# Tiny matmuls at the head of the TensorE program, and a transpose issued ahead of the output weights: one change to a fused attention and SwiGLU kernel

## The chip, the cores and the metric

The kernel runs on one core of one Trainium2 chip. A core has five engines that run their own programs and meet at semaphores: TensorE (PE in the profile) multiplies matrices into PSUM, VectorE (DVE) and ScalarE (ACT) work on SBUF and PSUM, GpSimd (POOL) works on SBUF, and SyncE (SP) issues transfers. PEld is TensorE's loading of the stationary operand. Transfers between HBM and SBUF run on 16 DMA engines; here nearly all loads and all DMA transposes are issued from SP's queue, in the order of its program, and the results from ScalarE's.

The metric is the device time in microseconds of the whole kernel, the median of several runs.

## What is computed

The inputs are q, k and v of 4 batches, 8 heads, 768 positions and 64 features, a decay `lam` per head, and three weight matrices: gate and value (512 x 1536) and out (1536 x 512). The reference runs an attention without softmax in blocks of 64 positions, with a state that decays, and then a gated feed-forward block:

```python
intra = np.einsum('bhic,bhjc->bhij', qb, kb) * Dmask[None]      # Dmask = lam ** (i - j), i >= j
intra = np.einsum('bhij,bhjd->bhid', intra, vb)
inter = np.einsum('bhid,bhde->bhie', qb * lam_pow[None], kv_state)
out[:, :, sl] = intra + inter
kv_state = lam_block * kv_state + np.einsum('bhsd,bhse->bhde', kb * rev_pow[None], vb)
...
g = x @ w_gate                                                   # x: attention output, 3072 x 512
return (g * (1.0 / (1.0 + np.exp(-g))) * (x @ w_val)) @ w_out
```

The 3072 rows are the 4 x 768 positions, the 512 columns the 8 heads of 64 features.

## The kernel before

The attention is cut into 12 groups of 256 positions of one batch; the state of a batch is carried from its group i to its group i + 1. Two groups make one tile t of 512 rows of the feed-forward block, so there are six tiles. The order of the work is written out by hand: nothing is scheduled by a planner. Each engine executes its instructions in the order in which this code issues them, so a call that is moved is moved on every engine that it uses.

One group g goes through these calls:

- `load_group` (L243): k, q and v from HBM by SP (L99 for groups 0 to 5, L106 for later ones).
- `cast_scaled` (L255): ScalarE casts k (L258), VectorE or GpSimd scales q (L260), and then SP issues `dma_transpose` (L248, L251) of both into `qkt`. Groups 0 to 2 use `pe_transpose` on TensorE (L289) in its place.
- `v_scale` (L235, L238): GpSimd scales v into `v_s`.
- `upd_mm` (L366, L382): TensorE forms the update of the state from k and `v_s`; `upd_copy` (L390) brings it to SBUF with ScalarE; `state` (L410, L421 to L432) adds it up on GpSimd and leaves `kvn`, the state in the middle of the group.
- `scores` (L308, L326): TensorE forms q times k; VectorE multiplies by the causal mask (L333).
- `core_a` (L490) with `inter` (L450, L461): q times the state, on TensorE, with `kv` and `kvn`; `core_b` (L495) with `intra` (L467, L474): scores times `v_s`; then `evac` (L481) copies the result to `xt`, the input of the feed-forward block. `ahead(g)` (L555) is `upd_mm`, `upd_copy`, `state` and `scores` in one.

The feed-forward block of tile t has 12 steps fc. A step is `ffn_gate` (L508, matmuls L514, silu on ScalarE L518) and `ffn_val` (L520, matmuls L528, product on VectorE L531), which give `h`. Then `ffn_out(t, b)` (L538, matmuls L547, copy L549, store L550) multiplies `h` by w_out for each of four blocks b of 128 rows, 12 matmuls each; matmul fc needs columns fc of w_out. Steps are numbered by `step` (L671), and `at(n, fn, ...)` (L675) hangs a call behind step n. The loop at L766 issues step after step and what hangs behind it. s0 are the steps of tile 0; tile 1 runs its 12 steps twice, on the first half of its rows (s1a) and on the second (s1b).

The weights come as float32 and are cast to bfloat16 in the core: gate and value in pieces by `w_piece` and `w_cast` (L206, L218), on ScalarE and GpSimd; out in six pieces of 512 KB by `wo_piece` and `wo_cast` (L225, L230), pieces 0 to 4 on GpSimd and piece 5 on ScalarE (L735). Before the change all six are issued at step s1a[3] behind the loads of group 5, and `cast_scaled(5)`, with its transpose, follows at s1b[3]. On GpSimd the order at the end of tile 1 is: pieces 0 and 1, `state(4)`, pieces 2 and 3, `v_scale(5)`, piece 4.

At the head, `warm_up` (L127) issues matmuls of 128x512 on constants. Four of them lead TensorE's program, then comes `lam_ps` (L163), a product that spreads `lam` over the partitions and from which ScalarE makes the decay tables, then three more. `warm_into` (L165) puts further matmuls on constants between the first stages. PSUM is used as a ring of eight banks.

The last call of the program, `ffn_out` with `last=True` (L542), splits its 512 columns: the first part is copied and stored by ScalarE, the second copied by VectorE and stored by SP.

Of the kernel before, what the change touches and what calls it, by code (L numbers as in the profile page):

```python
# [19 lines left out]
@with_exitstack  # L20
def kernel(
    ctx: ExitStack,
    tc: tile.TileContext,
    q: bass.AP,
    k: bass.AP,
    v: bass.AP,
    lam: bass.AP,
    moe_w_gate: bass.AP,
    moe_w_val: bass.AP,
    moe_w_out: bass.AP,  # L30
    out: bass.AP,
):
    nc = tc.nc
    with tc.manual_schedule():
        _body(ctx, tc, nc, q, k, v, lam, moe_w_gate, moe_w_val, moe_w_out, out)


def _body(ctx, tc, nc, q, k, v, lam, moe_w_gate, moe_w_val, moe_w_out, out):
    B, H, S, D = q.shape
# [3 lines left out]
    DM = H * D  # L43
    DFF = moe_w_gate.shape[1]
    MC = DM // 128
    FC = DFF // 128
# [32 lines left out]
    def bank():  # L79
        b = banks[ring[0] % 8]  # L80
        ring[0] += 1
        return b
# [41 lines left out]
    warm = nc.const_aps.tensor(1.0, [128, 512], BF16)  # L124
    ones = const.tile([1, 128], FP32, name="ones")
    nc.vector.memset(ones, 1.0)
    def warm_up(n, cols=512):  # L127
        b = bank()
        for _ in range(n):
            nc.tensor.matmul(b[:, 0:cols], warm[:, 0:128], warm[:, 0:cols], start=True, stop=True)  # L130
# [28 lines left out]
           for b in range(B)]  # L159

    lam_ps = bank()
    warm_up(4)
    nc.tensor.matmul(lam_ps[:, 0:H], ones[:, 0:128], lam_row, start=True, stop=True)  # L163
    warm_up(3)
    def warm_into(b, n, cols=256):  # L165
        for _ in range(n):
            nc.tensor.matmul(b[:, 0:cols], warm[:, 0:128], warm[:, 0:cols], start=True, stop=True)
# [370 lines left out]
    def ffn_out(t, b, last=False):  # L538
        h_sb = st[("h", t)]
        osb = osb_pool.tile([128, DM], FP32, name="osb", tag="osb")  # L540
        row = groups[2 * t + b // 2][0] * S + (groups[2 * t + b // 2][1] * 2 + b % 2) * BLK
        halves = ((0, DM // 2, nc.scalar.copy, nc.scalar), (DM // 2, DM, nc.vector.tensor_copy, nc.sync)) \  # L542
            if last else ((0, DM, nc.scalar.copy, nc.scalar),)
        for c0, c1, fn, eng in halves:
            ps = bank()[:, 0:c1 - c0]
            for fc in range(FC):
                nc.tensor.matmul(ps, h_sb[:, fc, b], wo_sb[:, fc, c0:c1],  # L547
                                 start=(fc == 0), stop=(fc == FC - 1))
            fn(out=osb[:, c0:c1], in_=ps)  # L549
            eng.dma_start(out=bass.AP(tensor=out.tensor, offset=out.offset + row * DM + c0,  # L550
                                      ap=[[DM, 128], [1, c1 - c0]]),
                          in_=osb[:, c0:c1])
# [118 lines left out]
    def step(t, fc, b0=0, b1=B):  # L671
        steps.append((t, fc, b0, b1))
        return len(steps) - 1

    def at(n, fn, *a):  # L675
        plan.setdefault(n, []).append((fn, a))

    s0 = {fc: step(0, fc) for fc in range(2, FC - 1)}
# [5 lines left out]
    at(s0[3], swapped_q_table)  # L684
    at(s0[4], w_cast)
    at(s0[4], state, 1)
    at(s0[4], load_group, 2, "v")
    at(s0[5], load_group, 3)
    at(s0[6], w_cast)
    at(s0[7], load_group, 4, "kq")  # L690
# [2 lines left out]
    at(s0[8], pe_transpose, 2, 0)  # L693
    at(s0[8], pe_transpose, 2, 1)
    at(s0[8], w_cast)
    at(s0[8], v_scale, 2, nc.gpsimd)
    at(s0[9], scores, 2)
    at(s0[9], run_later, 4)
    at(s0[10], upd_mm, 2)
# [7 lines left out]
    s1a = [step(1, fc, 0, 2) for fc in range(FC)]  # L707
    s1b = [step(1, fc, 2, 4) for fc in range(FC)]
    at(s1a[3], cast_scaled, 4)
    at(s1a[3], load_group, 5)  # L710
    for c in range(0, FC, 2):
        at(s1a[3], wo_piece, c, c + 2)
    at(s1a[7], scores, 3, (0,))
    at(s1a[7], run_later, 2)
    at(s1a[8], scores, 3, (1,))
# [4 lines left out]
    at(s1a[10], core_b, 3, SPLIT)  # L720
    at(s1a[10], v_scale, 4, nc.gpsimd)
    at(s1a[10], state, 3)
    at(s1b[3], cast_scaled, 5)
    at(s1b[3], load_group, 6)
    at(s1b[4], wo_cast)
    at(s1b[4], wo_cast)
    at(s1b[6], ahead, 4)
    at(s1b[6], run_later, 2)
    at(s1b[6], wo_cast)
    at(s1b[6], wo_cast)  # L730
    at(s1b[6], v_scale, 5, nc.gpsimd)
    at(s1b[8], wo_cast)
    at(s1b[9], core_a, 4)
    at(s1b[10], core_b, 4)
    at(s1b[10], wo_cast, ACTC)  # L735
    at(s1b[11], ffn_out, 0, 0)
    at(s1b[11], ahead, 5)
    at(s1b[11], run_later, 3)
    at(s1b[11], ffn_out, 0, 1)
    at(s1b[11], core_a, 5)  # L740
    at(s1b[11], ffn_out, 0, 2)
    at(s1b[11], core_b, 5)
    at(s1b[11], cast_scaled, 6)
# [62 lines left out]
```

## Time and profile before

| what | value |
|---|---|
| median of 13 runs | 228.37 us |
| lowest to highest | 227.87 to 230.0 us |
| the profiled execution: its own time | 229.31 us |
| its span, first to last instruction | 227.6 us |
| TensorE busy | 218.6 us (96%) |
| VectorE, ScalarE, GpSimd busy | 89.5, 107.4, 88.0 us |
| HBM read, written | 28.31 MB, 6.29 MB |
| granted TensorE clock, mean | 0.997 |

The profile is of one execution. Times in it count from the first instruction. A line of a timeline reads: start, length, engine, line of the kernel, operation, output from inputs, shape, how many instructions are put together, and in brackets how long the engine was idle before and what ended that. SPq and ACTq are the engines' queues of transfer issues; the length there is the time of the issue, and the landing of the data comes later. "issue" as a cause is time in which an engine waited for nothing that the profile shows. Busy time of TensorE includes the overlap of neighbouring matmuls, so a busy TensorE can still be sped up or slowed down. The profile also has a row for each 40th of the span, with the share of the DMA engines: they are busy without a break from the second slice to the twelfth (5.7 to 68 us), and mostly under half busy afterwards.

### The profile page before, as it was taken

To read this page: it belongs to the slowest core of one execution; us is meant where nothing else is said; L and a number is where in the kernel's file an instruction comes from. 1 tells how busy PE (TensorE), PEld (TensorE's weight loads), DVE (VectorE), ACT (ScalarE), POOL (GpSimd) and SP (SyncE) were. 2 spreads that over 40 slices of the span, in tenths; PEclk is the share of its full clock that TensorE was granted. 3 is DMA by queue.
4 is the path that set the end of the run, shared out by engine and by line. 5 is a ranking of instruction groups with operands and counts; after the bars stand their busy time and mean duration, and the time that the engine had idled before them with its cause. 6 is when DMAs were issued, how large, how long until landed. Compare 5 with 4: busy or idle time off the path is not lost.

```text
span 227.6 us, 5902 instructions
## 1 busy us (share of the span) xinstructions
PE 218.6 (96%) x2443; PEld 118.1 (52%) x2443; DVE 89.5 (39%) x151; ACT 107.4 (47%) x209; POOL 88.0 (39%) x131
## 2 busy tenths in 40 slices
PE   8789999999997999999999999999999999999994
PEld 3556456878853544454544544544544444444443
DVE  2664347685924213644352361353242123222200
ACT  5868585745562446454354363454433423322221
POOL 6676737641595132976373092092160000000000
PEclk9999999999999999999999999999999999999998
DMA  6999999999997877878889748915101101101122
GB/s 195 346 360 382 366 356 296 213 243 311 348 202 182 235 161 193 200 169 210 201 197 201 190 96 193 229 42 138 49 3 48 46 3 46 46 0 46 49 92 92
DMA packets 88012, 39.70 MB, mean 174 GB/s; under 512 B 57650, under 2 KB 83506, under 8 KB 87986
## 3 DMA queue, kind: packets, MB, share of 16 engines
q1 hardware_dynamic: 83474, 32.64, 55.4%
q10 hardware_dynamic: 4512, 6.69, 8.2%
q8 instruction: 19, 0.31, 0.6%
q14 instruction: 7, 0.06, 0.1%
HBM read 28.31 MB, written 6.29 MB: 152 GB/s over the span
## 4 chain that ended last, share of the span: by engine, by line
PE 82%; DMA 5%; SPq 5%; POOL 5%; issue 1%; ACT 0%; DVE 0%; DVEq 0%; POOLq 0%
PE bank L547 27%; PE bank L514 25%; PE bank L528 24%; SPq L99 4%; DMA woraw<-in_moe_w_out_dram 3%; DMA v<-in_v_dram 2%; POOL wo_sb L232 2%; POOL v_s L238 2%; PE bank L474 2%; PE bank L461 2%; PE bank L382 1%; PE bank L352 1%; SPq L227 1%; POOL kvf L421 1%; PE bank L326 0%
## 5 line engine op out<-in xcount | busy, mean ns | idle before, releaser
L531 DVE TENSOR_TENSOR h<-sil,bank 128x512 bf16<-128x512 bf16 (+1 forms) x87 | 51.3, 595 | 106.2 <-PE bank L528 90.4
L514 PE MATMUL bank<-xt,wg_sb 128*128 128x512 bf16 (+1 forms) x348 | 76.6, 343 | 0.0
L528 PE MATMUL bank<-xt,wv_sb 128*128 128x512 bf16 (+1 forms) x348 | 76.4, 342 | 0.0
L547 PE MATMUL bank<-wo_sb,h 128*128 128x512 bf16 (+1 forms) x300 | 65.8, 371 | 1.8 <-POOL wo_sb L232 1.8
L518 ACT ACTIVATE sil<-bank 128x512 bf16<-128x512 f32 (+1 forms) x87 | 45.8, 527 | 44.3 <-PE bank L514 41.3
L528 PEld LDWEIGHTS <-wv_sb 128*128 128x128 bf16 x348 | 34.0, 98 | 28.3
L547 PEld LDWEIGHTS <-h 128*128 128x128 bf16 x300 | 29.1, 98 | 34.3 <-issue 2.1
L514 PEld LDWEIGHTS <-wg_sb 128*128 128x128 bf16 x348 | 32.4, 98 | 27.2 <-DVE xt L486 0.3
L549 ACT COPY osb<-bank 128x512 f32<-128x512 f32 (+1 forms) x24 | 13.9, 577 | 54.5 <-PE bank L547 52.5
L238 POOL TENSOR_TENSOR v_s<-v,dec 128x1024 bf16<-128x1024 f32 (+1 forms) x14 | 23.3, 1667 | 16.3 <-DMA v<-in_v_dram 13.3
L421 POOL TENSOR_TENSOR kvf<-kvs,ups 128x256 f32<-128x256 f32 x8 | 5.8, 727 | 42.5 <-ACT ups L404 42.5
L333 DVE TENSOR_TENSOR ssb<-bank,causal 128x512 bf16<-128x512 f32 x24 | 15.3, 684 | 4.1 <-PE bank L326 4.0
L486 ACT CAST xt<-bank 128x512 bf16<-128x512 f32 x21 | 12.8, 663 | 2.9 <-PE bank L474 2.4
L430 POOL CAST kvn<-kvf 64x256 bf16<-64x256 f32 x24 | 12.5, 519 | 1.5
L421 POOL TENSOR_TENSOR kvf<-kvf,ups 128x256 f32<-128x256 f32 x16 | 11.6, 726 | 0.7
L260 DVE TENSOR_TENSOR qk<-qraw,qdn 128x1024 bf16<-128x1024 f32 x6 | 7.8, 1306 | 7.1 <-DMA qraw<-in_q_dram 3.7
L404 ACT COPY ups<-bank 128x256 f32<-128x256 f32 (+1 forms) x24 | 9.5, 449 | 2.4 <-PE bank L382 1.5
L258 ACT CAST qk<-kraw 128x1024 bf16<-128x1024 f32 x9 | 9.4, 1042 | 0.5 <-DMA kraw<-in_k_dram 0.5
L357 DVE TENSOR_TENSOR ssb<-bank,causaln 128x512 bf16<-128x512 f32 x12 | 8.3, 688 | 1.2 <-PE bank L352 1.1
L232 POOL CAST wo_sb<-woraw 128x1024 bf16<-128x1024 f32 x5 | 5.2, 1042 | 7.3 <-DMA woraw<-in_moe_w_out_dram 7.3
L221 POOL CAST wv_sb<-wraw 128x1024 bf16<-128x1024 f32 (+1 forms) x6 | 5.8, 971 | 5.3 <-DMA wraw<-in_moe_w_val_dram 5.2
L474 PE MATMUL bank<-ssb,v_s 64*64 64x128 bf16 (+1 forms) x384 | 6.8, 208 | 0.5 <-ACT guard L445 0.5
(63 smaller groups left out, 116.7 us busy)
## 6 DMA issues: line engine op xcount, KB each, us to landing
out_dram<-osb ACTq DMA_DIRECT2D x23, 256.0 KB, 2.1
v<-in_v_dram SPq DMA_DIRECT2D x16, 256.0 KB, 4.2
woraw<-in_moe_w_out_dram SPq DMA_DIRECT2D x6, 512.0 KB, 8.6
kraw<-in_k_dram SPq DMA_DIRECT2D x24, 128.0 KB, 3.4
qraw<-in_q_dram SPq DMA_DIRECT2D x24, 128.0 KB, 3.7
wraw<-in_moe_w_gate_dram SPq DMA_DIRECT2D x5, 512.0 KB, 7.2
wraw<-in_moe_w_val_dram SPq DMA_DIRECT2D x5, 512.0 KB, 6.9
kraw<-in_k_dram SPq DMA_DIRECT2D x4, 512.0 KB, 7.0
```

The costliest lines, as they stand in the source:

```text
L238: eng.tensor_tensor(out=st[("vs", g)][:, h0:h1], in0=st[("v", g)][:, h0:h1].rearrange("p h (s d) -> p h s d", s=2), in1=vfac(g, h0, h1), o ...
L333: nc.vector.tensor_tensor(out=ssb[:, h2, 2 * c:2 * c + 2].rearrange("p a s n -> p a (s n)"), in0=sp[(c, h2)].rearrange("p (a x) -> p a x", ...
L421: nc.gpsimd.tensor_tensor(out=o, in0=f, in1=u, op=ALU.add)
L430: nc.gpsimd.tensor_copy(out=o[64 - h2 * 64:128 - h2 * 64], in_=f[h2 * 64:h2 * 64 + 64])
L474: nc.tensor.matmul(op[r][h2 * 64:h2 * 64 + 64, cols(g, hp, s)], v_s[ps, 2 * hp + h2, s], ssb[ps, h2, hp * 2 + s] if g >= NAT0 else ssb[ps, ...
L486: fns[r](out=xt[:, g % 2, :, r].rearrange("p h (m s) -> p h s m", s=2) if g < NAT0 else xt[:, g % 2, :, :, r * M:r * M + M], in_=op[r].rea ...
L514: nc.tensor.matmul(gp[:, 0:N], wg_sb[:, mc, fs], xt[:, b0 // 2:b1 // 2, mc].rearrange("p g b n -> p g (b n)"), start=(mc == 0), stop=(mc = ...
L518: nc.scalar.activation(sil[:, 0:N], gp[:, 0:N], AF.Silu)
L528: nc.tensor.matmul(vp[:, 0:N], wv_sb[:, mc, fs], xt[:, b0 // 2:b1 // 2, mc].rearrange("p g b n -> p g (b n)"), start=(mc == 0), stop=(mc = ...
L531: nc.vector.tensor_tensor(out=h_sb[:, fc, b0:b1].rearrange("p b n -> p (b n)"), in0=sil[:, 0:N], in1=vp[:, 0:N], op=ALU.mult)
L547: nc.tensor.matmul(ps, h_sb[:, fc, b], wo_sb[:, fc, c0:c1], start=(fc == 0), stop=(fc == FC - 1))
L549: fn(out=osb[:, c0:c1], in_=ps)
```

## The change

There are five edits.

- At the head, four matmuls of 128x512 are replaced by 78 matmuls with a stationary operand of 64x64 and 8 moving columns, on the lower and upper half of the rows in turn; the lam product follows directly, and five matmuls of 128x512 (before: three) follow that.
- `load_group(2, "v")` becomes two loads of half the heads, and `v_scale(2)` becomes two instructions of half the heads.
- Only piece 0 of w_out is issued at s1a[3]. `cast_scaled(5)`, with the transpose of group 5, moves from s1b[3] to s1b[0]; pieces 1 to 5 of w_out follow behind it, then the loads of group 6.
- `v_scale(5)` moves behind the last w_out cast on GpSimd.
- The last store is split at column 384 instead of 256.

On GpSimd the order at the end of tile 1 becomes: pieces 0 and 1, `state(4)`, pieces 2, 3 and 4, `v_scale(5)`. On SP it becomes: loads of group 5, piece 0, transpose of group 5, pieces 1 to 5, loads of group 6. TensorE's program grows from 4,885 to 5,037 instructions.

```diff
     lam_ps = bank()
-    warm_up(4)
+    b = bank()
+    for n in range(78):
+        r = slice(n % 2 * 64, n % 2 * 64 + 64)
+        nc.tensor.matmul(b[r, 0:8], warm[r, 0:64], warm[r, 0:8], start=True, stop=True, skip_group_check=True)
     nc.tensor.matmul(lam_ps[:, 0:H], ones[:, 0:128], lam_row, start=True, stop=True)
-    warm_up(3)
+    warm_up(5)
...
-        halves = ((0, DM // 2, nc.scalar.copy, nc.scalar), (DM // 2, DM, nc.vector.tensor_copy, nc.sync)) \
+        halves = ((0, DM - 128, nc.scalar.copy, nc.scalar), (DM - 128, DM, nc.vector.tensor_copy, nc.sync)) \
             if last else ((0, DM, nc.scalar.copy, nc.scalar),)
...
-    at(s0[4], load_group, 2, "v")
+    at(s0[4], load_fp32, 2, nc.sync, v, "v", 0, H // 2)
+    at(s0[4], load_fp32, 2, nc.sync, v, "v", H // 2, H)
...
-    at(s0[8], v_scale, 2, nc.gpsimd)
+    at(s0[8], v_scale, 2, nc.gpsimd, 0, H // 2)
+    at(s0[8], v_scale, 2, nc.gpsimd, H // 2, H)
...
     at(s1a[3], cast_scaled, 4)
     at(s1a[3], load_group, 5)
-    for c in range(0, FC, 2):
-        at(s1a[3], wo_piece, c, c + 2)
+    at(s1a[3], wo_piece, 0, 2)
...
-    at(s1b[3], cast_scaled, 5)
-    at(s1b[3], load_group, 6)
+    at(s1b[0], cast_scaled, 5)
+    for c in range(2, FC, 2):
+        at(s1b[0], wo_piece, c, c + 2)
+    at(s1b[0], load_group, 6)
     at(s1b[4], wo_cast)
     at(s1b[4], wo_cast)
     at(s1b[6], ahead, 4)
     at(s1b[6], run_later, 2)
     at(s1b[6], wo_cast)
     at(s1b[6], wo_cast)
-    at(s1b[6], v_scale, 5, nc.gpsimd)
     at(s1b[8], wo_cast)
+    at(s1b[8], v_scale, 5, nc.gpsimd)
```

## The prediction

> **What bounds the kernel now.** I read the busy shares first, then what TensorE (PE) waits for, then the chain that ended last, then the timelines around the places the diff names. PE is busy 218.6 of the 227.6 us span, and the table of stretches puts its idle time before 16 us (3.3 us), between 48 and 70 us (1.8 us) and in crumbs of about 0.3 us a group after that. So a change pays only where PE stands still, and a new PE wait is paid in full. PE's own waits:
>
> ```profile
> engine line waited for: us in total, times, longest us
> PE bank L547 <- POOL wo_sb L232: 1.8, 1, 1.8
> ...
> PE bank L167 <- issue: 0.7, 1, 0.7
> ```
>
> The large one is the first output product (`ffn_out(0, 0)`, L547) waiting for the fifth cast piece of w_out. The chain that ended last (start, length, what) shows what that wait stands on:
>
> ```profile
> 53.03 7.54 DMA woraw<-in_moe_w_out_dram
> 60.63 1.04 POOL wo_sb L232
> 61.67 0.70 POOL kvf L421
> ...
> 66.63 1.88 POOL v_s L238
> 68.50 0.99 POOL wo_sb L232
> 69.54 1.02 PE bank L547 x4
> ```
>
> The landing of piece 1 of w_out (53.03 + 7.5 = 60.5) starts a stretch in which GpSimd (POOL) never rests until 69.49: cast of piece 1, state of group 4, pieces 2 and 3, v scale of group 5, piece 4. SP's own timeline in that stage, transposes (L251), loads (L99) and w_out pieces (L227):
>
> ```profile
> 41.36 2.10 SPq L251 DMA_TRANSPOSE qkt<-qk  x1
> 43.53 0.57 SPq L99 DMA_DIRECT2D v<-in_v_dram  x1
> 45.67 2.25 SPq L251 DMA_TRANSPOSE qkt<-qk  x1
> 47.96 0.59 SPq L99 DMA_DIRECT2D kraw<-in_k_dram  x1
> ...
> 51.59 4.62 SPq L227 DMA_DIRECT2D woraw<-in_moe_w_out_dram  x6
> 58.51 8.16 SPq L251 DMA_TRANSPOSE qkt<-qk  x1
> ```
>
> Today all six pieces are issued ahead of group 5's transpose. The same stage on POOL and PE, where the state of group 4 is handed over:
>
> ```profile
> 62.42 0.40 POOL L432 CAST kvn<-kvf 128x256 bf16<-128x256 f32 x1
> 62.81 0.30 PE L461 MATMUL bank<-qkt,kv 64*64 64x128 bf16 x2
> 62.89 0.22 PE L461 MATMUL bank<-qkt,kvn 64*64 64x128 bf16 x1
> ```
>
> `kvn` is done at 62.82 and PE uses it at 62.89. There is no slack between piece 1 and PE.
>
> **The change, part by part. 1: w_out behind the transpose.** Five pieces move on SP's queue past one transpose, and that transpose waits for `cast_scaled(5)`, which moves from step s1b[3] to s1b[0]. VectorE (DVE) finishes the product of s1b[0] at 54.62; q of group 5 was issued at 48.61 and lands 6.0 later, 54.6. So its scaling (1.22) ends at 55.84, and by the row of 44.31 + 1.22 -> 45.67 the transpose is issued 0.14 later, 55.98. SP then has nothing to issue from 52.99 to there. ScalarE's cast of k (landed 48.0 + 5.2 = 53.2) fits at 54.07; the eight PSUM banks let PE run about three steps (2.6 us) ahead of both engines, so it doesn't feel the 1.2 us.
>
> The issue of a transpose takes 2.1 to 2.25, so piece 1 can't be issued before about 58.1 (53.03 today). When does it land? Two rows show a 512 KB load issued directly behind a transpose: v of group 4, 41.36 -> 43.53 + 4.4 = 47.9, that is 6.5 after the transpose's issue; k of group 5, 45.67 -> 53.2, that is 7.5, with more loads behind it as here. I take the middle, 7.0. Part 2 brings the casts 0.2 forward, so the transpose is issued at 55.8 and piece 1 lands at **62.8 (62.3 to 63.3)** instead of 60.5.
>
> POOL's program waits for it in order: behind cast 1 stand the state of group 4, casts 2 to 4 and now last the v scale. Two things follow. `kvn` comes 2.3 after the landing (62.82 - 60.53), at 65.1, and PE, due at `inter(4)` at 62.6, stands about 2.5 us. That isn't the end of it, since POOL is the engine behind: from the start of cast 1 to the end of the stretch it works 8.86 today (60.63 to 69.49), the same instructions in the new order. With 0.1 from landing to start and 0.05 to PE, the v scale is done and `upd_mm(5)` (L382) starts at landing + 9.0 = **71.8**. Today it starts at 70.49. The later stall takes in the earlier: PE, 2.5 us late, reaches the output product at 68.1, finds piece 4 cast at 69.9, just when its turn comes, ends it near 70.7, and waits 1.1 more for the v scale. Pieces 2 to 4 land about 1.4 us apart and are cast later than that; piece 5, on ScalarE, lands near 68.5, is cast by about 69.7 and used at 70.2.
>
> Cost: 71.8 - 70.49 = **+1.3**, bounds +0.8 and +1.8 by the two rows. No PE wait behind 71 us can give it back (the idle there is 2.5 us in 156, inside the groups). The transposed group 5 comes at about 60 instead of 70.3, and the group 6 loads leave SP earlier; both only gain slack, since `scores(5)` at 70.9 didn't wait.
>
> **Cast before v scale (POOL).** By itself it would remove the 1.77 wait, and then `upd_mm(5)` would wait for the v scale instead, due at 69.49: at most 0.95 won. Its whole effect is in the 9.0 above.
>
> **2: the head.** PE stops for no cause shown at 13.9 to 14.73, and further on is bound by a cast:
>
> ```profile
> 14.73 0.27 PE L167 MATMUL bank<-const-bfloat16-1.0 128*128 128x256 bf16 x1 [0.68 <-issue]
> 18.98 1.04 POOL L221 CAST wv_sb<-wraw 128x1024 bf16<-128x1024 f32 x1 [2.06 <-DMA wraw<-in_moe_w_val_dram]
> 20.33 1.03 PE L528 MATMUL bank<-xt,wv_sb 128*128 128x512 bf16 x4
> ```
>
> The instruction queue moved 19 packets, 0.31 MB, for 4,886 PE instructions, 257 each, and the first packet inside the span lies in the stretch 12.0 to 13.3, just ahead of the stop. So I read the stop as PE running out of fetched instructions. The change puts 152 more instructions ahead, which moves the same boundary to the scores of group 1 (10.97). PE stood 256 instructions ahead of the old place at 9.56, only 4.2 us before it was due there; for the new place it is 5.4 us and 5.6. So the stop should go or shrink. But the cast at 18.98 waits for a transfer in a stretch where the DMA moves 345 GB/s without a break from 3 us on; it ends at 20.02, PE uses it at 20.33. So of 0.7 to 0.9 at most 0.27 is kept.
>
> Against that stands the time of the 78 products: they replace four of 128x512 (0.84 to 2.64 with the wait for the fourth to drain). The nearest row is `upd_mm`: 32 products of 64x64 in four quarters of the array in 0.45, 14 ns each. With two quarters and the halved pace of the cold array (the 512-column ones here take 427 ns, later 216), I estimate 28 ns a product with its load, 2.2 us: the lam product moves from 2.64 to about 3.0. The Trainium skill, TensorE: Matmul & The Clock Gate, "Wait — 56ns, not 53.3ns?", speaks of a floor of about 25 ns from start to start, or 62 ns where the sequencer decodes in software; 62 would make 4.8 us and the lam product 3 us late. The 14 ns of this trace speaks against 62, so I keep 28. 0.4 later runs through ScalarE's tables, but v of group 1 (landing 11.3) and its scaling to 13.41 cover it. The v load and v scale of group 2 in halves: one more issue (0.7, under transfers that already queue) and 2.06 against 1.92 on POOL; ready at about 36.3 instead of 36.61, where PE takes it at 36.67, so the 0.27 gets through. Value 0.2, bounds -0.5 (late tables) and 0.3; it is inside the 55.8 above and not added again.
>
> The same page ("What's actually happening") gives the clock's window as about 3.4 us of inactivity. The 1.8 us stop of today left the clock at 1.0; two stops of 2.5 and 1.1 stay under the rule too. If tiny products don't count as activity, the clock, today up at 4.6 us, rises a window later; with cold work up to 8 us I put that at 0.5 to 1 at `upd_mm(5)`. By the row: nothing; by the rule's bad case: 230.3.
>
> **3: the tail.** 384 + 128 columns instead of 256 + 256. First half 12 x 162 ns = 1.95 from 221.63 on, second 12 x 56 ns (16 transposes of 128 columns take 0.89) = 0.67: PE ends within 0.05 of today. DVE copies 128 columns in about 0.28 instead of 0.42, so SP issues at 224.57 instead of 224.76; ScalarE's piece is issued at 224.1 and is not last. **-0.2.**
>
> **Sum.** +1.3 - 0.2 = +1.1 on the profiled execution: span 227.6 -> 228.7, its own time 229.31 -> 230.4. That execution is 0.9 above the median of 228.37, so I set the difference on the median: **229.5**.
>
> **Rivals.**
> *B, a wash.* Piece 1 lands at 61.5 to 62.0, as v of group 4 suggests with larger packets (2 KB against 512 bytes). `upd_mm(5)` at 70.5 to 71.0, less the tail: 228.2 to 228.7. For it: one of two rows nearly; against it: the pieces behind.
> *C, faster.* The transpose doesn't hold the pieces up. If piece 1 landed by 60.5, `upd_mm(5)` would start at 69.5, 1.0 earlier, with the tail 227.2; at best, with the v scale off the path, 68.6 and 226.3. It decides from a landing before 61.0. Against it: SP issue at 57.9 plus the shortest landing of 512 KB in this stage, 4.4, is already 62.3.
> *D, a slow head.* Tiny products at 62 ns or a clock that rises late, on top of part 1: about 231.
> *No effect* would need piece 1 off POOL's path, and the chain shows it on it.
>
> **How the numbers follow.** Sum 0.57 (own range 228.9 to 230.2), B 0.20, C 0.09, D 0.14. A measurement here tells about 0.3%, 0.7 us, from no change. Slower: D and most of the sum, 0.66; same: B and the low end of the sum, 0.24; faster: C and a little of B, 0.10. The range 228.2 to 231.0 leaves out C and the far end of D.
>
> **What would show it.** Right: the transpose of group 5 issued near 55.8, the first cast behind it on POOL near 62.9, a PE wait of about 2.5 us for `kvn` in front of L461 of group 4, a second of 1 us for the v scale, L547 without its 1.8. No stop of PE near 14. Wrong: piece 1 cast before 61.5, PE waiting in the head, or a granted clock below 1.0 after 5 us.

## The result, and the profile after

| | before | after |
|---|---|---|
| median | 228.36 us (48 runs) | 231.18 us (11 runs, 230.72 to 232.23) |
| ratio | | 1.0122, 95% interval 1.0103 to 1.0142 |
| profiled execution: own time, span | 229.31, 227.6 us | 233.85, 232.1 us |

The change costs 2.8 us; 229.5 (228.2 to 231.0) had been forecast. The profiled execution is slower than the eleven behind the median: its mean clock is 0.992, theirs 0.998 to 1.0, and the stretch at half clock behind this shows below. The new head adds three lines to the code, so L461 before is L464 here, L547 is L550 and L382 is L385.

In TensorE's waits the 1.8 us for `wo_sb` in front of the output product is gone, and this heads the list (total us, times, longest us):

```profile
PE bank L464 <- POOL kvn L435: 3.1, 1, 3.1
```

The chain of work that ended last (start, length, what) shows what that wait stands on:

```profile
60.44 0.50 SPq L254
60.99 4.88 DMA woraw<-in_moe_w_out_dram
65.92 1.04 POOL wo_sb L235
66.96 0.69 POOL kvf L424
67.71 0.41 POOL kvn L435
68.16 1.06 PE bank L464 x15
...
72.70 2.59 PE bank L550 x12
75.29 0.38 PE bank L385 x32
```

Piece 1 of w_out is issued behind the transpose, lands at 65.9, and holds up GpSimd's cast, the state and `inter(4)`, the order that the prediction gave. `upd_mm(5)` (L385) starts at 75.3 instead of 70.5. SP's timeline shows where the lateness begins:

```profile
43.34 2.83 SPq L254 DMA_TRANSPOSE qkt<-qk  x1
...
54.05 1.64 SPq L230 DMA_DIRECT2D woraw<-in_moe_w_out_dram  x1
59.30 1.64 SPq L254 DMA_TRANSPOSE qkt<-qk  x1
60.99 3.66 SPq L230 DMA_DIRECT2D woraw<-in_moe_w_out_dram  x5
```

The transpose of group 3 (43.34, before 41.36) is already 2.0 late, 17 us ahead of the first moved piece of w_out (60.99). That comes from the head: `e1_head_only` below, which moves no piece, issues it at 43.76. The transpose of group 5 leaves at 59.3, not at the predicted 55.8. GpSimd from there:

```profile
60.63 1.04 POOL L235 CAST wo_sb<-woraw 128x1024 bf16<-128x1024 f32 x1 [6.05 <-DMA woraw<-in_moe_w_out_dram]
65.92 1.04 POOL L235 CAST wo_sb<-woraw 128x1024 bf16<-128x1024 f32 x1 [4.25 <-DMA woraw<-in_moe_w_out_dram]
...
69.89 3.02 POOL L235 CAST wo_sb<-woraw 128x1024 bf16<-128x1024 f32 x3
72.86 1.92 POOL L241 TENSOR_TENSOR v_s<-v,dec 128x1024 bf16<-128x1024 f32 x1
```

GpSimd works without a rest from 65.92 to 74.78, 8.86 us, as long as before. And the table of stretches has a clock that did not stay up. A row reads: from and to, length, busy us of TensorE, of its weight loads, of VectorE, ScalarE and GpSimd (in brackets how many instructions), granted clock, DMA share, GB/s.

```profile
64.42:67.83 3.41, 0.62 (x6) 0.26 (x3) 1.02 (x3) 0.38 (x1) 1.85 (x3) 1.00 1.00 371
67.83:71.24 3.41, 3.08 (x35) 2.11 (x39) 0.09 (x1) 0.54 (x2) 3.27 (x6) 0.50 1.14 348
71.24:74.65 3.41, 3.41 (x50) 2.09 (x43) 0.65 (x2) 2.52 (x4) 3.41 (x3) 1.00 0.52 113
```

TensorE worked for only 0.62 of the 3.41 us of the first stretch and had half its clock (0.50) in the next 3.41 us.

### The profile page after: what moved, and what is told of

Its sections match the earlier page's. It is cut to its first block, busy times and chain, and to the rows that moved or that the text cites. A ratio compares the mean times of both kernels' runs of the same rounds, so it can differ in the third digit from the quotient of the medians.

```text
span 232.1 us, 6055 instructions
## 1 busy us (share of the span) xinstructions
PE 222.3 (96%) x2519; PEld 120.5 (52%) x2519; DVE 89.5 (39%) x151; ACT 107.1 (46%) x209; POOL 90.7 (39%) x132
## 4 chain that ended last, share of the span: by engine, by line
PE 81%; DMA 9%; SPq 7%; POOL 1%; issue 1%; ACT 0%; DVE 0%; DVEq 0%
PE bank L550 27%; PE bank L517 24%; PE bank L531 23%; DMA qraw<-in_q_dram 4%; SPq L99 4%; DMA wraw<-in_moe_w_val_dram 3%; SPq L216 3%; DMA woraw<-in_moe_w_out_dram 2%; PE bank L464 2%; PE bank L477 2%; PE bank L385 1%; PE bank L355 1%; PE bank L329 1%; PE bank L292 1%; POOL wo_sb L235 0%
## 5 line engine op out<-in xcount | busy, mean ns | idle before, releaser
L550 PE MATMUL bank<-wo_sb,h 128*128 128x512 bf16 (+2 forms) x300 | 65.6, 371 | 0.0
L550 PEld LDWEIGHTS <-h 128*128 128x128 bf16 x300 | 28.7, 98 | 32.9
L424 POOL TENSOR_TENSOR kvf<-kvf,ups 128x256 f32<-128x256 f32 x16 | 13.4, 841 | 0.6
L464 PE MATMUL bank<-qkt,kvn 64*64 64x64 bf16 (+1 forms) x192 | 5.9, 205 | 3.1 <-POOL kvn L435 3.1
```

What stands on the lines that cost most here:

```text
L424: nc.gpsimd.tensor_tensor(out=o, in0=f, in1=u, op=ALU.add)
L464: nc.tensor.matmul(op[r][h2 * 64:h2 * 64 + 64, cols(g, hp, s)], kv[n][dp, hp], tt[dp, 1, s, hq, rm] if g >= NAT0 else tt[dp, 1, :, hp, rm] ...
L550: nc.tensor.matmul(ps, h_sb[:, fc, b], wo_sb[:, fc, c0:c1], start=(fc == 0), stop=(fc == FC - 1))
```

## The experiments

Every ratio is to the kernel before, timed beside it on the same chip; the interval behind it is the 95% interval. Theory S put the loss into the w_out stage, theory H a good part of it into the head.

### The parts alone

`e1_head_only` is the kernel before with the new head:

```diff
-    warm_up(4)
+    b = bank()
+    for n in range(78):
+        r = slice(n % 2 * 64, n % 2 * 64 + 64)
+        nc.tensor.matmul(b[r, 0:8], warm[r, 0:64], warm[r, 0:8], start=True, stop=True, skip_group_check=True)
     nc.tensor.matmul(lam_ps[:, 0:H], ones[:, 0:128], lam_row, start=True, stop=True)
-    warm_up(3)
+    warm_up(5)
```

> The kernel before with the new head alone (78 tiny products, lam product, five of 512 columns). Theory S, the loss sits in the w_out stage: this run stays within 0.4 us of before, 228.0 to 228.8, because the 0.4 us by which the lam product is later is covered by the wait for v of group 1. Theory H, the head carries a good part of the loss, as the profile of the change shows it (group 2's transposes on TensorE at 33.4 instead of 31.6): 229.5 to 230.5.

Measured: 229.98 us, ratio 1.0058 (1.0036 to 1.0081): the head alone costs 1.3 us.

`e2_wo_only` is the kernel before with pieces 1 to 5 of w_out behind the transpose of group 5, its cast at s1b[0], and the v scale last on GpSimd; no new head, no split tail:

```diff
-    for c in range(0, FC, 2):
-        at(s1a[3], wo_piece, c, c + 2)
+    at(s1a[3], wo_piece, 0, 2)
...
-    at(s1b[3], cast_scaled, 5)
-    at(s1b[3], load_group, 6)
+    at(s1b[0], cast_scaled, 5)
+    for c in range(2, FC, 2):
+        at(s1b[0], wo_piece, c, c + 2)
+    at(s1b[0], load_group, 6)
...
-    at(s1b[6], v_scale, 5, nc.gpsimd)
     at(s1b[8], wo_cast)
+    at(s1b[8], v_scale, 5, nc.gpsimd)
```

> The kernel before with the moved pieces of w_out, the earlier cast and transpose of group 5, and the v scale of group 5 last on GpSimd; head, halves of v and tail as before. Theory S: 230.5 to 231.7, with a TensorE wait of about 3 us for kvn in front of L461 and a stretch of half clock behind it. Theory H: 229.0 to 229.8, the 1.3 of the written sum and no more.

Measured: 230.91 us, ratio 1.0095 (1.006 to 1.0131). The chain of its profiled execution is the prediction's working with other numbers:

```profile
58.13 4.54 DMA woraw<-in_moe_w_out_dram
...
62.73 1.04 POOL wo_sb L232
...
64.52 0.40 POOL kvn L432
...
66.69 3.01 POOL wo_sb L232 x3
69.70 1.88 POOL v_s L238
...
71.62 0.45 PE bank L382 x32
```

Its TensorE waits:

```profile
PE bank L461 <- POOL kvn L432: 1.5, 1, 1.5
PE bank L382 <- POOL v_s L238: 1.2, 2, 0.8
```

Without the head's 0.2 and the tail the prediction's terms give a landing at 63.0, `upd_mm(5)` at 72.0, 1.5 later than before, and an own time of 229.31 + 1.5 = 230.8; measured were 62.7, 71.6 and 230.41. Yet the whole loss is 2.2 (by the ratio). The clock of each execution tells why: the three that ran at 1.0 took 229.8, 229.8 and 230.4 us; the three at 0.993 took 231.4, 231.9 and 232.1. By these few executions the order of transfers costs 1.3 us (by the middle one of the three) to 1.5 (by their mean) at full clock, and 1.8 more by the means where the clock was down. That price fits 3.41 us at half speed (3.41 / 2 = 1.7).

`e3_all_but_wo` is the change with the w_out pieces and `cast_scaled(5)` put back where they were (the edits of `e2_wo_only` undone, except the v scale's place):

> The changed kernel with the order of SP's queue undone (all six pieces of w_out ahead of the transpose of group 5, cast of group 5 at s1b[3]); the v scale of group 5 stays last on GpSimd. Theory S: faster than before, 227.0 to 227.9, as the TensorE wait of 1.8 us shrinks by up to 0.95 and the tail gains 0.2. Theory H: 228.7 to 229.8.

Measured: 229.44 us, ratio 1.0033 (1.0014 to 1.0051), inside theory H's range. Against the whole change (1.0122) the w_out order is worth 0.9%, 2.0 us, in the presence of the new head. `after_again` is the whole change once more, beside the later kernels:

> The changed kernel once more, beside the other runs of this chip: 230.7 to 231.7. Its profile tells which of the two prices, the thin loads between 8 and 18 us and the half clock behind the wait for kvn, comes with every execution: theory F has the thin loads each time; the half clock may be missing, since the kernel with the filled wait was no faster.

Measured: 232.81 us over six runs, ratio 1.0182 (1.0138 to 1.0226), above what was expected. Three runs at a clock of 0.998 to 1.0 took 231.0, 232.1 and 232.8; three at 0.992 to 0.993 took 232.9, 234.1 and 234.4, so the half clock stood in half of them and lifts the median. Neither theory alone is right: head and w_out order each cost over 1 us.

### The w_out stage: which wait, and which move

`e4_pool_only` changes only GpSimd's order:

```diff
-    at(s1b[6], v_scale, 5, nc.gpsimd)
     at(s1b[8], wo_cast)
+    at(s1b[8], v_scale, 5, nc.gpsimd)
```

> The kernel before with one edit, the v scale of group 5 behind the last w_out cast on GpSimd. Both theories: the wait of L547 for piece 4 (1.8 us) goes, upd_mm(5) then waits for the v scale until about 69.5 instead of starting at 70.5: 227.3 to 227.8. If the v scale on the path costs as much as the cast did: 228.2 to 228.5.

Measured: 228.25 us, ratio 0.9985 (0.9968 to 1.0001). The gain of 0.3 is not clear of zero, and smaller than both theories had expected (227.3 to 227.8). In its profile the 1.8 us wait at L547 is gone.

`e5_state_first` is the change with the state of group 4 ahead of the cast of piece 1, so that `kvn` no longer hangs on the landing:

```diff
-    at(s1b[4], wo_cast)
     at(s1b[6], ahead, 4)
     at(s1b[6], run_later, 2)
+    at(s1b[6], wo_cast)
```

> The changed kernel with one edit: on GpSimd the state of group 4 goes ahead of the cast of w_out piece 1. Theory S: the TensorE wait of about 3 us for kvn is gone and with it the half clock; the v scale of group 5 still ends about 9 us behind the landing of piece 1 less the 2.9 us of the state, so it is no longer late. Expected 228.9 to 229.8, which is the changed kernel (231.2) less 1.5 to 2.3, and what remains above before is the head. If the late piece 1 hurts in another way than through kvn: 230.5 to 231.5.

Measured: 232.25 us, ratio 1.0161 (1.0105 to 1.0216), above both ranges. Three of its six runs had the half clock again (0.991 to 0.993); the three at full clock took 230.7, 231.4 and 231.5, as the change does (median 231.2). So there is no gain. The wait for `kvn` is gone from its list, and others have come at the output product:

```profile
PE bank L550 <- ACT wo_sb L235: 1.7, 1, 1.7
...
PE bank L550 <- POOL wo_sb L235: 0.8, 1, 0.8
```

So `kvn` is only the first to notice. The pieces themselves are late, and with the state out of the way TensorE waits for the last of them, the one that ScalarE casts.

`e8_fill` is the change with eight matmuls of 128x512 on constants ahead of `inter(4)`, into a bank that is overwritten afterwards, to keep TensorE working through the wait:

```diff
         st[("op", g)] = [bank() for _ in range(2)]
+        if g == 4:
+            warm_into(st[("op", g)][0], 8, 512)
```

> The changed kernel with eight products of 512 columns on constants (1.7 us) put in front of inter of group 4, where TensorE waits for kvn; their result is overwritten. If the half clock behind that wait costs time in most runs: faster than the changed kernel by 0.5 to 1.5, 229.7 to 230.7, and no stretch of half clock in the profile. If the clock costs nothing there, because TensorE would wait for the v scale anyway: the same as the changed kernel, 231.0 to 231.4.

Measured: 231.75 us, ratio 1.013 (1.0087 to 1.0172). All six runs had a clock of at least 0.998, where three of the six beside it in `after_again` had not, so the fill goes with the absence of the half-clock stretch. Its runs (230.8 to 232.1) are no shorter than the full-clock runs of the change (230.7 to 232.8 in the two series): the late pieces remain, and its profile has a wait of 1.1 us for the piece that ScalarE casts.

`e10_cast_early` moves the cast and transpose of group 5 to s1b[0] as the change does, but leaves all six pieces ahead of the transpose:

```diff
-    at(s1b[3], cast_scaled, 5)
-    at(s1b[3], load_group, 6)
+    at(s1b[0], cast_scaled, 5)
+    at(s1b[0], load_group, 6)
...
-    at(s1b[6], v_scale, 5, nc.gpsimd)
     at(s1b[8], wo_cast)
+    at(s1b[8], v_scale, 5, nc.gpsimd)
```

> The kernel before with the cast and transpose of group 5 at s1b[0] instead of s1b[3], all six pieces of w_out still ahead of the transpose on SP's queue, and the v scale last on GpSimd. It differs from the moved pieces (230.9) only in what stands in front on SP's queue. Theory S, the pieces behind the transpose make the cost: 228.0 to 228.6, as with the GpSimd order alone (228.25). If the earlier cast on ScalarE and VectorE makes it: 230 to 231.

Measured: 227.86 us, ratio 0.9966 (0.9948 to 0.9984). It differs from `e2_wo_only` only in SP's order, and stands 0.0129 below it. SP and GpSimd in its timelines:

```profile
52.25 5.30 SPq L227 DMA_DIRECT2D woraw<-in_moe_w_out_dram  x6
57.71 8.30 SPq L251 DMA_TRANSPOSE qkt<-qk  x1
```

```profile
60.41 1.04 POOL L232 CAST wo_sb<-woraw 128x1024 bf16<-128x1024 f32 x1 [0.20 <-DMA woraw<-in_moe_w_out_dram]
```

Piece 1 is cast at 60.4 instead of 62.7 in `e2_wo_only`. The loss of the w_out part is the place of five pieces behind one transpose, and nothing else in it.

### The head: the late product, or the longer program

The head had been priced at a gain. Two accounts of its loss were left: theory L, that the lam product comes too late, and theory F, that TensorE's longer program moves the transfers of its instruction packets into the early loads. `e6_lam_late` delays the lam product to 3.07 with large warm-up products and adds three of them, 6 TensorE instructions in all with their weight loads (not the 8 of the expectation):

```diff
-    warm_up(4)
+    warm_up(5)
     nc.tensor.matmul(lam_ps[:, 0:H], ones[:, 0:128], lam_row, start=True, stop=True)
-    warm_up(3)
+    warm_up(5)
```

> The kernel before with five products of 512 columns ahead of the lam product instead of four, and five behind it instead of three: the lam product at about 3.06 us and the first transposes at about 5.6, as with the 78 tiny products, but only 8 more TensorE instructions instead of 152. Theory L, the late lam product and the late first transposes cost the head's 1.3 us: 229.3 to 230.2. Theory F, the shifted fetch of instructions costs it, by landing in the loads of group 1 at 8 us: 228.2 to 228.8, with 0.69 MB in each 2 us up to 12 us.

Measured: 228.81 us, ratio 1.002 (0.9993 to 1.0047), a mixture again: thirteen runs at a clock of 0.998 or more took 228.1 to 229.4 us, twelve of them below 229; nine at 0.990 to 0.991 took 229.8 to 231.0. With the clock up, a late lam product costs nothing. The half clock is in its profile too, behind a stop of TensorE of 1.1 us:

```profile
13.07:16.48 3.41, 2.06 (x84) 1.50 (x85) 2.06 (x4) 1.97 (x5) 2.19 (x5) 1.00 1.12 365
16.48:19.89 3.41, 3.41 (x25) 2.16 (x22) 1.15 (x2) 1.27 (x3) 1.33 (x2) 0.50 1.09 383
```

`e9_tiny2` and `e7_tiny30` are `e1_head_only` with 2 and with 30 tiny products. With 2 the program has as many instructions as before (2,443 weight loads in both profiles, and one matmul for each); with 30 it has 56 more, with 78 it has 152 more.

> The kernel before with the new head, but 2 tiny products instead of 78: as many TensorE instructions as before, so the first instruction packet inside the span stays near 12.3 us; the lam product as early as its data allow, five products of 512 columns behind it. Theory F (the place of the instruction packets in the stream of loads makes the head's cost): 228.1 to 228.7 and no thin stretch of loads between 8 and 20 us. If the new head costs time in another way: 229.3 to 230.3, as with 78 and with 30.

> The kernel before with the new head, but 30 tiny products instead of 78 (56 more instructions instead of 152). The first instruction packet inside the span should move from 12.3 to about 11.5 us, behind the last load of group 1's v, not to 8. Theory F: 228.0 to 228.8 and no slow transfers between 10 and 18 us. If tiny products hurt by themselves or the five products behind the lam product do: 229.2 to 230.2.

Measured: with 2, 228.84 us, ratio 1.0005 (0.9987 to 1.0023); with 30, 230.24 us, ratio 1.0066 (1.0043 to 1.009), as much as with 78. So the loss does not grow with the tiny products' number or time, and the five products behind lam, which both kernels have, are not its cause. Lam comes at 2.1 us in both, earlier than before: theory L has no account of the loss with 30. But theory F had forecast none there either. Its form, that the packet harms only among the loads of group 1, was wrong; the packet did move as forecast, to 11.6 us.

`e12_lam_first` puts the 78 tiny products behind the lam product, which comes at 2.64 as before; the program is 156 longer:

```diff
     warm_up(4)
     nc.tensor.matmul(lam_ps[:, 0:H], ones[:, 0:128], lam_row, start=True, stop=True)
+    b = bank()
+    for n in range(78):
+        r = slice(n % 2 * 64, n % 2 * 64 + 64)
+        nc.tensor.matmul(b[r, 0:8], warm[r, 0:64], warm[r, 0:8], start=True, stop=True, skip_group_check=True)
     warm_up(3)
```

> The kernel before with the 78 tiny products put behind the lam product instead of ahead of it; the four 128x512 products still lead, so lam comes at 2.64 as before. Theory L (a late lam product is the head's price): no loss, 228.2 to 228.8 where before is 228.4. Theory F (the place of TensorE's instruction packets among the loads): the first packet still moves from about 12.3 to about 8 us, the transfers of 12 to 18 us slow as with the new head, and the time is 229.4 to 230.4.

Measured: 230.24 us, ratio 1.0078 (1.0047 to 1.0109). Lam is on time and the loss is there: theory L is out. Theory F's forecast held here. In the stretches of 12 to 18 us (last number: GB/s) the kernel before has

```profile
12.00:14.00 2.00, 1.66 (x58) 1.14 (x57) 2.00 (x6) 2.00 (x6) 1.96 (x3) 1.00 1.15 338
14.00:16.00 2.00, 1.32 (x38) 0.79 (x36) 0.74 (x2) 0.44 (x3) 1.06 (x2) 1.00 1.11 374
16.00:18.00 2.00, 2.00 (x25) 1.69 (x24) 0.77 (x2) 1.55 (x4) 0.79 (x2) 1.00 1.09 385
```

and `e1_head_only`

```profile
12.00:14.00 2.00, 1.75 (x61) 1.40 (x49) 1.42 (x5) 1.79 (x6) 1.79 (x3) 1.00 1.03 301
14.00:16.00 2.00, 1.89 (x83) 1.24 (x72) 1.58 (x3) 1.50 (x4) 1.75 (x3) 1.00 0.92 238
16.00:18.00 2.00, 2.00 (x25) 1.54 (x24) 1.15 (x2) 1.31 (x4) 1.23 (x2) 1.00 0.95 273
```

The change moves 265, 256 and 315 GB/s there, `e12_lam_first` 315, 256 and 317; `e7_tiny30` falls clearly behind only from 16 us on (335, 359, 314). `e9_tiny2`, which costs nothing, moves 343, 368 and 385, and `e6_lam_late` 343, 370 and 385. So the loads are slower in each of these four kernels with a head that costs, and not in the two with one that doesn't.

SP's timelines show where it starts. TensorE's first instruction packet in the stream lies at 12.3 us in the kernel before and at 13.0 with 2 tiny products, but at 11.6 with 30 and at 7.6 to 8.1 with 78, and takes 0.9 us. In all sixteen traces the SP issue that falls into this time is 0.8 to 1.6 us longer than others of its kind; a lone weight piece mostly takes 0.69 at that point. In the change this meets v of group 1, whose two issues take 3.0 us in place of 1.59, so the first weight piece is issued at 9.84 instead of 8.42:

```profile
6.79 3.00 SPq L99 DMA_DIRECT2D v<-in_v_dram  x2
9.84 0.66 SPq L216 DMA_DIRECT2D wraw<-in_moe_w_gate_dram  x1
```

With 30 tiny products it meets the fifth weight piece (first line), in the kernel before the sixth (second line), with 2 the seventh (13.05, 1.50 long):

```profile
11.42 1.93 SPq L216 DMA_DIRECT2D wraw<-in_moe_w_gate_dram  x1
12.11 1.87 SPq L213 DMA_DIRECT2D wraw<-in_moe_w_val_dram  x1
```

So every kernel here has such a long issue; what differs is which transfers stand behind it.

What `e1_head_only` makes of the late loads are two waits of TensorE for a weight cast, 0.9 us together:

```profile
PE bank L531 <- POOL wv_sb L224: 0.9, 2, 0.5
```

Its `upd_mm(2)` comes at 39.06 (before 36.67), 2.4 late, of which the old wait for w_out takes up a part: `upd_mm(5)` is 1.0 late. All this fits theory F, that the packet's place among the loads sets the price. It isn't shown: no run moved a packet and nothing else, and no run made the program longer by anything but tiny products. `e12_lam_first` even has another path in its profile: TensorE is 1.2 late at 17 us without waiting for weights, and then stops for no cause shown in front of the output product, where the wait for w_out had been (`e3_all_but_wo` has such a stop of 1.8 us):

```profile
68.70 2.53 PE L551 MATMUL bank<-wo_sb,h 128*128 128x512 bf16 x11 [1.46 <-issue]
```

So the loss goes with the longer program, not with a late lam; which of its effects decides in the median stays open. One trace shows one execution only: the profiled one of `e7_tiny30` (229.34) is 0.9 faster than its median.

### What is left to gain

`e11_pool_tail` is the kernel before with GpSimd's new order, the tail split at 384, and v of group 2 in halves; `e13_best` adds the early cast of `e10_cast_early`.

> The kernel before with the three edits that have not shown a cost: the v scale of group 5 last on GpSimd, the last store split at column 384, and the v load and v scale of group 2 in halves. If the gains add up (0.25 of the first, 0.27 of the second as read in the profiles): 227.7 to 228.1, faster than before by 0.3 to 0.6.

> The kernel before with the scaling of q and k of group 5 moved to s1b[0], all six pieces of w_out still ahead of its transpose, the v scale of group 5 last on GpSimd, the last store split at 384 and v of group 2 in halves; old head. e10_cast_early stood at 0.9966 and e11_pool_tail at 0.995. If the early scaling and the tail add up: 0.9925 to 0.995, about 226.8 where before is 228.4. If both only show the change of GpSimd's order: 0.995 to 0.997.

Measured: `e11_pool_tail` 227.20 us, ratio 0.995 (0.9928 to 0.9972); `e13_best` 227.66 us, ratio 0.995 (0.993 to 0.997). Both are faster than before and after. `e11_pool_tail` gains 1.1, twice what its parts had been expected to give. The early cast adds nothing to the rest.

## Why the prediction was wrong

**The w_out order** was right in mechanism and size. The transpose of group 5 went at 56.27 in `e2_wo_only` (55.98 predicted without the head), its piece 1 landed 6.4 later (6.6 in the change; 7.0 taken, 6.5 to 7.5 allowed), and landing to `upd_mm(5)` took 8.9 (9.0). At full clock the part costs 1.3 to 1.5, for a +1.3. The sentence "the later stall takes in the earlier" held in `e2_wo_only`: TensorE waits 1.5 for `kvn`, again 0.8 for the v scale, and the chain runs through the v scale. With the new head it is not so: in the change's profile the v scale is done at 74.78 and TensorE comes for it only at 75.2, and in `e5_state_first` and `e8_fill` TensorE waits for ScalarE's piece of w_out instead. That piece the prediction had taken as cast in time.

**The head is the step that failed.** It was valued at a gain of 0.2 (worst case a loss of 0.5); alone it measured a loss of 1.3 (0.8 to 1.9). Its parts were partly right. The stop near 14 us is gone, and the 78 products took 2.18 us (0.84 to 3.02), 28 ns each, the estimate's figure and not the 62 weighed against it. That match is luck in part. The working names two reasons to double the 14 ns of `upd_mm`, half as many quarters and half the pace, and doubles once. But the 14 also holds the drain of the last product: the trace has the 32 starts within 0.25 us, 8 ns apart, and 8 doubled twice is 32. What was left out is the other side of "the change moves the same boundary": I followed what an earlier packet does for TensorE, and not what happens to the loads. I had also written that the DMA moves 345 GB/s without a break, and didn't draw the conclusion that whatever disturbs that stream delays the weights behind it. The working even took "v of group 1 (landing 11.3)" as fixed cover for late tables. GpSimd's scaling of that v, before and in the change, shows that the landing itself moved by 1.4:

```profile
11.35 2.06 POOL L238 TENSOR_TENSOR v_s<-v,dec 128x512 bf16<-128x512 f32 x2
12.71 2.06 POOL L241 TENSOR_TENSOR v_s<-v,dec 128x512 bf16<-128x512 f32 x2 [0.22 <-DMA v<-in_v_dram]
```

The worst case only knew late tables, which `e12_lam_first` excludes. What the runs put in the place of the gain is a loss of 1.3 to 1.8 that comes with the longer program; that the instruction packet among the loads makes it fits the traces and is not proven.

And the lateness does not stay within the head: the transpose of group 5, now ahead of five w_out pieces, hung on it. It left at 59.30 in the change's profile, 3.5 later than predicted, and at 57.2 to 58.4 in `e5_state_first`, `e8_fill` and `after_again`, which have the same head; without the new head (`e2_wo_only`) at 56.27. Before, a late TensorE could use up the 1.8 us wait at L547.

**The clock** was valued at nothing, by the rule of the Trainium skill (TensorE: Matmul & The Clock Gate, "What's actually happening") that about 3.4 us of inactivity lower it, against stops of 2.5 and 1.1. The runs don't bear the rule out as I used it: the half clock followed a stop of 3.1 us in the change, and one of 1.1 us in `e6_lam_late`. It costs about 1.8 us where it occurs, in half of the executions of `e2_wo_only`. The eleven runs behind the median of 231.18 had the clock at 0.998 or more, so it is no part of the 2.8; the sum at full clock is 1.3 for the head, 1.3 to 1.5 for w_out and the tail's -0.3, 2.3 to 2.5 of 2.8. The other 0.3 to 0.5 is not assigned, and it is 0.8 to 1.0 if tail and v halves together are taken at -0.8, the distance of `e11_pool_tail` from `e4_pool_only`. The intervals of the terms are half a us and more, so this rest is not clear of noise; that the head now delays the transpose, and through it the pieces, is a candidate that no run isolates.

**The tail** was right: from the start of the last output matmul to the end of the span 3.66 us before, 3.38 after; -0.2 was predicted. VectorE's copy takes 0.29 (0.28) and SP issues last:

```profile
228.32 0.48 ACT L552 COPY osb<-bank 128x384 f32<-128x384 f32 x1 [1.36 <-PE bank L550]
...
229.05 0.29 DVE L552 COPY osb<-bank 128x128 f32<-128x128 f32 x1 [9.69 <-DMA out_dram<-osb]
229.37 0.37 SPq L553 DMA_DIRECT2D out_dram<-osb  x1
```

**GpSimd's order** by itself: "at most 0.95 won", measured 0.3 (0 to 0.7), inside. **The v halves** were not run alone; in `e11_pool_tail`, which has them, nothing is lost.

**The rivals.** B and C fell with the landing of 62.7 where they needed 62.0 and 61.0. D, "a slow head", has the right total (about 231) for the wrong reasons. Tiny products of 62 ns are out, at 28. A clock that rises late is out too: by the traces' records of the granted clock it rises at 6.4 us in the change (4.6 before), but at 8.1 in `e9_tiny2` and at 9.2 in `e10_cast_early`, which lose nothing.

## What to carry to other kernels

When instructions are added at the head of an engine's program, price the stream of loads as well as the engine: the kernels with a longer TensorE program lost 1.3 to 1.8 us, whether with 30 or 78 tiny products and with lam early or late, while a new head of equal length was free. A load of 512 KB put behind a transpose on the same queue landed 5.6 to 7.5 us after the transpose's issue in these traces, so what TensorE waits for first belongs ahead of it. And a stop of TensorE is to be priced with the clock that may follow, even a short one.

## What the runs showed of the hardware

The half-clock stretches inside the span are each 3.41 us long (the change, `after_again`, `e6_lam_late`) and lie on a grid counted from the moment when the clock first rises. By the traces' own records of the granted clock it rises at 6.39 in the change and falls at 67.83, 18.0 stretches later; in `e6_lam_late` it rises at 6.24 and falls at 16.48, 3.0 later. Where the grid lies differs from execution to execution, not with the head: the clock first rises anywhere from 4.1 to 9.2 in the six traces with the old head. So the same stop of TensorE can meet the grid differently each time, which may be why only some executions of a kernel lose the clock.

TensorE was busy for 0.62 us of the stretch ahead in the change and for 2.06 in `e6_lam_late`. A busy share alone doesn't decide: on the same grid the kernel before has a stretch (66.03 to 69.44) with 1.73 us busy and kept its clock. What does is open.

TensorE's instruction packets are rare and large: 19 of them, 0.31 MB, in the change, so one of 16 KB for some 260 instructions. In the DMA table of 7.5 to 9 us one of them has 3.9% of 16 engines' time, 1.5 x 16 x 0.039 = 0.9 us on its engine (queue and kind, packets, MB, share):

```profile
q8 instruction: 1, 0.02, 3.9%
```
